# At most three streamed weight loads under way, and one streamed pair moved from the v to the q projection, in a recurrent attention kernel

## The chip, the cores and the metric

The kernel runs on one core of one Trainium2 chip. The metric is the time of one execution on the device in microseconds (us), lower is better. A change counts as faster or slower when it moves the time by more than 2%; verdicts come from several runs with a 95% interval. A ratio below is the mean time of one kernel's fast runs over that of the other's fast runs of the same rounds, so it is not quite the ratio of the medians that are quoted beside it.

Names: PE is the matmul engine, ACT, DVE and POOL are the other compute engines, SP is the engine that issues most of the DMAs here, in program order. The profile prints times in us.

## The reference, cut to what matters

```python
for s in range(n_seg):                         # 64 segments of 32 tokens, one after the other
    xs = x[:, s * 32:(s + 1) * 32, :]
    h = concatenate([mem, xs], axis=1)         # 8 memory rows + 32 rows
    q, k, v = h @ Wq, h @ Wk, h @ Wv           # 1024 -> 32 heads x 128
    p = softmax(where(mask, q k^T * scale, -1e9))
    o = (p v) @ Wo                             # 32 x 128 -> 1024
    mem = o[:, :8, :]                          # the next segment needs this
    outs.append(o[:, 8:, :])
b = gelu(x @ w_gate) * (x @ w_up) @ w_down     # a dense stage, independent of the loop
return g * a + (1 - g) * b                     # a: the concatenated outs; g: a sigmoid gate of x, cut here
```

All in bfloat16. Each segment needs all four weights, 8 MB each, 32 MB in all. That is more than fits on the chip beside the rest. So most of the weights stay resident and a part is streamed from HBM again in every segment.

## The kernel before

The weights are cut into 64 pieces of 512 KB: four matrices, two halves of the heads (r = 0 and 1), eight pieces i. Some pieces share a slot in pairs: piece i of one half and piece i of the other half take turns in one slot. The other pieces stay. There are 12 pairs (k 2, q 2, v 5, o 3), so each segment loads 12 pieces.

```python
PAIRS = {"k": (0, 2), "q": (0, 2), "v": (0, 1, 2, 4, 6), "o": (0, 2, 4)}

def seq(m, r):                       # order of the pieces in one projection half
    p = [i for i in range(8) if i in PAIRS[m]]
    f = sorted(...)                  # the others
    return p + f if r == 0 else f + p
ORDER = (("k", 0), ("q", 0), ("v", 0), ("k", 1), ("q", 1), ("o", 0), ("v", 1), ("o", 1))
walk = [(m, r, i) for m, r in ORDER for i in seq(m, r)]
```

In the first half (r = 0) the paired pieces come first; as soon as PE has used one, SP loads its partner into the slot; the partner is used at the very end of the second half (r = 1). The next segment begins with the half that is then in the slots, so there is one load per pair and segment.

```python
def fetch(n):
    k, t = uses[n][done[n]], slots[n]
    ...
    op("sp", lambda e: e.dma_start(dst(t, k), src(k)), wr=[t.r()], lane=lane)

def spent(k):                        # called after the matmuls that used piece k
    n = home[k]
    done[n] += 1
    if done[n] < len(uses[n]) and uses[n][done[n]] != k:
        fetch(n)
```

`op` works out from the regions read and written (`rd`, `wr`) which semaphores an instruction waits for; `after=` adds such a wait. So a load waits for PE's last use of its slot and for nothing else. One projection piece is 4 matmuls of 512 columns (k, q, v) or 8 of 256 columns (o), on four column groups of the array at once:

```python
for g in range(4):
    ins = e.matmul(PB[bk][32 * g:32 * g + 32, :], lhsT=h[:, i, :], rhs=w[:, g * 512:(g + 1) * 512],
                   start=(p % 8 == 0), stop=(p % 8 == 7))
```

Of the kernel before, what the change touches and what calls it, by code (L numbers as in the profile page):

```python
# [30 lines left out]
class _Prog:  # L31
# [47 lines left out]
    def op(self, eng, fn, rd=(), wr=(), lane=None, after=()):  # L79
        o = _Op(eng, fn)  # L80
        if lane is not None:
            ln = self.lanes.get(lane)
            if ln is None:
                ln = self.lanes[lane] = [self.new_sem(f"{self.name}_{lane}"), 0, None]
            if ln[2] is not None:
                o.deps.append(ln[2])
            ln[1] += 16
            o.sem, o.val, o.inc, o.need = ln[0], ln[1], 16, True
            ln[2] = o
        for r in rd:  # L90
            self._touch(o, r, False, lane is not None)
        for r in wr:
            self._touch(o, r, True, lane is not None)
        o.deps.extend(after)
        if eng == "pool" and lane is None:
            if self.pool is not None:
                o.deps.append(self.pool)
            self.pool = o
        for d in o.deps:
            d.need = True  # L100
        o.idx = len(self.ops)
        self.ops.append(o)
        return o
# [92 lines left out]
def bass_gated_mix__memory_aug_recurrent_mem_tr__geglu_ffn__prompt_kernel(  # L196
# [34 lines left out]
    with ExitStack() as es:  # L231
# [31 lines left out]
        def al(name, shape, dt=BF16, at=None):  # L263
            if at is None:
                cur[0] = (cur[0] + 63) // 64 * 64
                t = _T(nc, name, shape, dt, cur[0])
                cur[0] += t.nb
                return t
            return _T(nc, name, shape, dt, at)
# [12 lines left out]
        kT = al("kT", [128, 4, 4, LQ])  # L282
        qT = al("qT", [128, 4, 4, 32])
# [20 lines left out]
        NSLOT = NLOW + (top - cur[0]) // PIECE  # L304


        PAIRS = {"k": (0, 2), "q": (0, 2), "v": (0, 1, 2, 4, 6), "o": (0, 2, 4)}

        def seq(m, r):
            p = [i for i in range(8) if i in PAIRS[m]]  # L310
            f = sorted((i for i in range(8) if i not in p), key=lambda i: (m == "k" and i % 2, i))
            return p + f if r == 0 else f + p
# [3 lines left out]
        def at_step(p, s):  # L316
            m, r, i = walk[p]
            return (m, r ^ (s % 2), i)

        hosts = []  # L320
        for m in "kqvo":
            for i in range(8):
                if i in PAIRS[m]:
                    hosts.append([(m, 0, i), (m, 1, i)])
# [7 lines left out]
        for s_ in range(NSEG):  # L332
            for p in range(64):
                k = at_step(p, s_)
# [3 lines left out]
        op = P.op  # L338
# [3 lines left out]
        def src(k):  # L342
            m, u, i = k
            if m == "o":
                h0 = 16 * u + 2 * i
                return A_Wo[h0:h0 + 2].rearrange("h p f -> p h f")
            W = {"q": A_Wq, "k": A_Wk, "v": A_Wv}[m]
            return W[i * 128:(i + 1) * 128, 16 * u:16 * u + 16, :].rearrange("d h e -> d (h e)")

        def dst(t, k):  # L350
            return t[:, :].rearrange("p (h f) -> p h f", h=2) if k[0] == "o" else t[:, :]

        nlane = [0]
        done = [0] * len(hosts)

        def fetch(n):
            k, t = uses[n][done[n]], slots[n]
            if paired(k):
                lane = f"sl{n}"
            else:  # L360
                lane = f"res{nlane[0] % 8}"
                nlane[0] += 1
            op("sp", lambda e: e.dma_start(dst(t, k), src(k)), wr=[t.r()], lane=lane)

        def first(k):
            n = home[k]
            if done[n] == 0 and uses[n][0] == k:
                fetch(n)

        def spent(k):  # L370
            n = home[k]
            assert uses[n][done[n]] == k
# [3 lines that stand above are left out]
# [8 lines left out]
        for g in range(4):  # L384
            q = slice(32 * g, 32 * g + 32)
# [68 lines left out]
        def load_qk(s, r):  # L454
            u = r ^ (s % 2)
            op("pool", lambda e: e.dma_start(qkr[:, r, :, :], qk_scr[:, s, 2 * u:2 * u + 2, :]),
               rd=[("D", "qk", s // 4, 2 * u), ("D", "qk", s // 4, 2 * u + 1)], wr=[qkr.r(256 * r, 256 * r + 256)], lane=f"qkr{r}")

        def load_v(s, us=slice(0, 2)):
# [7 lines left out]
           wr=[gwb.r()], lane="gw")  # L467
# [90 lines left out]
        assert NSEG % 2 == 0  # L558
        lost = [("o", 1, i) for i in PAIRS["o"]]
        xo = {k: al(f"xo{k[2]}", [128, 2048], at=tail - (n + 1) * PIECE) for n, k in enumerate(lost)}  # L560
# [17 lines left out]
        def dve_copy(o, i, rd, wr):  # L578
            op("dve", lambda e: e.tensor_copy(o, i), rd=rd, wr=wr)  # L579
# [3 lines left out]
        def evac(bank, t):  # L583
            act_copy(t[:, :], PB[bank][:, :], [BK(bank)], [t.r()])
# [6 lines left out]
        def trans(to):  # L591
            op("pe", trans4, rd=[tok.r(), ident.r()], wr=[BK(TT)])
            i_ap = PBV[TT][:, 0:512].rearrange("p (j g c) -> p (j g) c", g=4, c=32)
            dve_copy(to[:, :, :, 0:32].rearrange("p j g c -> p (j g) c"), i_ap, [BK(TT)], [to.r()])
# [169 lines left out]
        for s in range(NSEG):  # L764
# [12 lines left out]
            def on(m, r, n, *fs):  # L777
                at.setdefault(base_of[m, r] + n, []).extend(fs)
# [27 lines left out]
            on("q", 0, 0, lambda: evac(bank_of["k", 0], tok))  # L806
            on("q", 0, 5, lambda: trans(kT))
            on("v", 0, 0, lambda: evac(bank_of["q", 0], tok))
            on("v", 0, 4, lambda: trans(qT))
            on("k", 1, 0, lambda: evac(bank_of["v", 0], vA))  # L810
            on("k", 1, 0, lambda: scores(0))
            on("k", 1, 3, lambda: rest_k(1))
# [1 line left out]
            if not last:  # L814
                on("q", 1, 0, lambda: load_h(s + 1))
                on("q", 1, 1, lambda: load_qk(s + 1, 0))
                on("v", 1, 2, lambda: load_qk(s + 1, 1))
            on("q", 1, 4, lambda: trans(kT))
            if s % 4 == 0 and Q >= 0:
                on("q", 1, 2, lambda: load_oR(Q, 1))  # L820
            if s % 4 == 1 and Q >= 0:
# [97 lines left out]
        for fb in range(NFB):  # L919
            HB, DN = ((0, 1, 2, 3), (4, 5, 6, 7)) if fb % 2 == 0 else ((4, 5, 6, 7), (0, 1, 2, 3))  # L920
            for j in range(NJ):
# [13 lines left out]
                t = tp[j % 2]  # L935
# [76 lines left out]
```

## Time and profile before

The median was 2304 us. The recurrent stage is some 1520 us of it (62 of the 64 segments, from the first hand-over between segments to the last), the dense stage at the end about 645 us, the start about 140 us. A mean segment, from the trace's records (60 segments; times from the segment's start, in us):

| load | k | k | q | q | v | v | v | v | v | o | o | o | next segment |
|---|---|---|---|---|---|---|---|---|---|---|---|---|---|
| landed | 5.2 | 7.1 | 9.2 | 10.7 | 12.2 | 14.0 | 15.3 | 16.6 | 17.8 | 19.2 | 20.9 | 22.4 | 24.5 |
| first used | 8.1 | 8.4 | 10.4 | 11.0 | 17.8 | 18.0 | 18.3 | 18.5 | 18.9 | 22.6 | 22.9 | 23.3 | |

The stream is almost as long as PE's own work. These lines are from the page of the kernel before; in the rows each digit (or number) is one of 40 equal slices of the span, PE and DMA in tenths of busy time, GB/s as moved:

```profile
span 2304.5 us, 80168 instructions
PE   2588998899999998898998998998879999999998
DMA  9968788788788787787887887887782802606206
GB/s 358 379 213 305 257 304 294 261 289 309 265 303 302 272 316 271 269 322 265 290 323 248 302 302 256 302 303 266 270 330 90 276 34 80 230 1 208 103 1 237
```

Who PE waited for (who <- whom: us in total, times, longest us):

```profile
PE pb L682 <- issue: 46.1, 44, 2.3
...
PE pb L670 <- DMA sl<-in_A_Wq_dram: 18.4, 28, 1.6
...
PE pb L670 <- DMA sl<-in_A_Wv_dram: 7.9, 13, 1.0
...
PE pb L682 <- DMA sl<-in_A_Wo_dram: 7.6, 14, 1.0
```

L670 is a k, q or v projection piece, L682 an o piece. "issue" means that no semaphore explains the wait. The last number of the DMA issue lines is the median time from issue to landing:

```profile
sl<-in_A_Wv_dram SPq DMA_DIRECT2D x331, 512.0 KB, 9.9
sl<-in_A_Wo_dram SPq DMA_DIRECT2D x205, 512.0 KB, 5.9
sl<-in_A_Wk_dram SPq DMA_DIRECT2D x142, 512.0 KB, 5.5
sl<-in_A_Wq_dram SPq DMA_DIRECT2D x142, 512.0 KB, 7.4
```

The v pieces take 9.9 us because up to eight loads wait in line. The last view is the DMA view of one segment, 799.9 to 823.7 us, again in 40 slices (0.6 us each):

```profile
DMA  0037988999999999999999999999999999720120
GB/s 0 0 69 241 220 172 256 407 413 386 379 413 386 399 372 399 379 392 399 386 372 372 386 406 413 427 406 386 358 358 389 392 410 372 282 83 34 34 76 0
```

After a slow start of about 3 us (70 to 256 GB/s) the stream runs at about 390 GB/s until all 12 loads are in.

### The profile page before, as it was taken

To read this page: it belongs to the slowest core of one execution; us is meant where nothing else is said; L and a number is where in the kernel's file an instruction comes from. 1 tells how busy PE (TensorE), PEld (TensorE's weight loads), DVE (VectorE), ACT (ScalarE), POOL (GpSimd) and SP (SyncE) were. 2 spreads that over 40 slices of the span, in tenths; PEclk is the share of its full clock that TensorE was granted. 3 is DMA by queue.
4 is the path that set the end of the run, shared out by engine and by line. 5 is a ranking of instruction groups with operands and counts; after the bars stand their busy time and mean duration, and the time that the engine had idled before them with its cause. 6 is when DMAs were issued, how large, how long until landed. Compare 5 with 4: busy or idle time off the path is not lost.

```text
span 2304.5 us, 80168 instructions
## 1 busy us (share of the span) xinstructions
PE 2060.9 (89%) x36594; PEld 1099.2 (48%) x36614; DVE 901.2 (39%) x2164; ACT 604.1 (26%) x1280; POOL 616.0 (27%) x1107
## 2 busy tenths in 40 slices
PE   2588998899999998898998998998879999999998
PEld 1244555555555555555555455554444444444443
DVE  3134333334334343343343433333335164363452
ACT  1122232222323222232232322222223032131230
POOL 5233333343333433333333333333210000000000
PEclk9999999999999999999999999999999999999999
DMA  9968788788788787787887887887782802606206
GB/s 358 379 213 305 257 304 294 261 289 309 265 303 302 272 316 271 269 322 265 290 323 248 302 302 256 302 303 266 270 330 90 276 34 80 230 1 208 103 1 237
DMA packets 225714, 576.45 MB, mean 250 GB/s; under 512 B 30424, under 2 KB 42584, under 8 KB 225376
## 3 DMA queue, kind: packets, MB, share of 16 engines
q1 hardware_dynamic: 189536, 513.35, 61.7%
q0 software_dynamic: 26624, 44.14, 5.6%
q10 hardware_dynamic: 9216, 13.83, 1.7%
q8 instruction: 287, 4.70, 0.8%
q14 instruction: 51, 0.42, 0.1%
HBM read 539.71 MB, written 31.39 MB: 248 GB/s over the span
## 4 chain that ended last, share of the span: by engine, by line
PE 65%; DMA 24%; issue 5%; DVE 3%; ACT 2%; POOL 1%; SPq 0%; ACTq 0%; POOLq 0%; DVEq 0%
PE pb L670 20%; PE pb L929 14%; DMA sl<-in_A_Wq_dram 11%; PE pb L682 9%; PE pb L697 6%; PE pb L966 6%; DMA sl<-in_A_Wo_dram 5%; PE pb L712 3%; PE pb L588 3%; DMA sl<-in_A_Wv_dram 3%; DMA wd<-in_B_w_down_dram 2%; PE pb L609 1%; DMA xr_scr<-xr 1%; PE pb L641 1%; PE pb L603 1%
## 5 line engine op out<-in xcount | busy, mean ns | idle before, releaser
L670 PE MATMUL pb<-sl,hT 128*32 128x512 bf16 x12288 | 756.8, 383 | 43.2 <-DMA sl<-in_A_Wq_dram 18.4
L670 PEld LDWEIGHTS pb<-sl,hT 128*32 128x32 bf16 x12288 | 331.7, 97 | 327.2 <-DMA sl<-in_A_Wq_dram 38.8
L682 PE MATMUL pb<-sl,oT 128*32 128x256 bf16 x8192 | 281.8, 275 | 56.2 <-issue 46.1
L576 ACT ACTIVATE tok<-pb 128x512 bf16<-128x512 f32 x320 | 191.0, 597 | 458.0 <-PE pb L670 393.0
L682 PEld LDWEIGHTS pb<-sl,oT 128*32 128x32 bf16 x8192 | 213.0, 97 | 98.7 <-issue 54.6
L697 PE MATMUL pb<-sl,hR 128*32 128x512 bf16 x3072 | 215.0, 390 | 19.6 <-DMA sl<-in_A_Wq_dram 7.3
L929 PE MATMUL pb<-xT,wg 128*128 128x512 bf16 x896 | 213.2, 381 | 16.2 <-DVE GT L945 8.4
L655 POOL COPY oRc<-oT 128x128 bf16<-128x128 bf16 x128 | 98.6, 770 | 452.4 <-DVE oT L579 445.4
L929 PE MATMUL pb<-xT,wu 128*128 128x512 bf16 x896 | 211.7, 379 | 0.0
L966 PE MATMUL pb<-wd,GT 128*128 128x512 bf16 x876 | 194.7, 379 | 8.9 <-DMA wd<-in_B_w_down_dram 7.7
L579 DVE CAST oT<-pb 128x160 bf16<-128x160 f32 x256 | 71.2, 320 | 230.4 <-PE pb L646 230.4
L937 ACT ACTIVATE s<-pb 128x512 f32<-128x512 f32 x112 | 66.8, 596 | 326.8 <-PE pb L929 307.3
L929 PEld LDWEIGHTS pb<-xT,wg 128*128 128x128 bf16 x896 | 87.1, 98 | 125.1 <-DVE GT L945 12.8
L576 ACT ACTIVATE vA<-pb 128x512 bf16<-128x512 f32 x128 | 76.4, 597 | 265.9 <-PE pb L670 265.9
L966 PEld LDWEIGHTS pb<-wd,GT 128*128 128x128 bf16 x896 | 86.4, 98 | 117.2 <-DMA wd<-in_B_w_down_dram 15.5
L588 PE MATMUL pb<-ident,tok 128*128 128x128 bf16 x1280 | 128.1, 222 | 13.2 <-ACT tok L576 8.9
L929 PEld LDWEIGHTS pb<-xT,wu 128*128 128x128 bf16 x896 | 87.7, 98 | 105.9 <-issue 0.3
L938 DVE SCALAR_TENSOR_TENSOR tp<-s,pb 128x512 f32<-128x512 f32 x112 | 76.9, 687 | 155.2 <-ACT s L937 155.1
L588 PEld LDWEIGHTS pb<-ident,tok 128*128 128x128 bf16 x1280 | 72.6, 98 | 123.2 <-ACT tok L576 94.3
L579 DVE COPY kT<-pb 128x512 bf16<-128x512 bf16 x128 | 51.9, 405 | 197.9 <-PE pb L588 197.9
L614 DVE TENSOR_REDUCE st<-pb 128x8 f32<-128x320 f32 x128 | 62.9, 492 | 159.6 <-PE pb L609 159.6
L697 PEld LDWEIGHTS pb<-sl,hR 128*32 128x32 bf16 x3072 | 83.3, 98 | 81.5 <-DMA sl<-in_A_Wq_dram 8.4
(76 smaller groups left out, 1929.7 us busy)
## 6 DMA issues: line engine op xcount, KB each, us to landing
sl<-in_A_Wv_dram SPq DMA_DIRECT2D x331, 512.0 KB, 9.9
sl<-in_A_Wo_dram SPq DMA_DIRECT2D x205, 512.0 KB, 5.9
sl<-in_A_Wk_dram SPq DMA_DIRECT2D x142, 512.0 KB, 5.5
sl<-in_A_Wq_dram SPq DMA_DIRECT2D x142, 512.0 KB, 7.4
wd<-in_B_w_down_dram SPq DMA_DIRECT2D x56, 1024.0 KB, 6.4
qk_scr<-stg POOLq DMA_DIRECT2D x64, 128.0 KB, 5.8
qkr<-qk_scr POOLq DMA_DIRECT2D x128, 64.0 KB, 5.4
wg<-in_B_w_gate_dram SPq DMA_DIRECT2D x3, 1792.0 KB, 13.2
```

The source lines that it names most:

```text
L576: op("act", lambda e: e.activation(o, i, ACTF.Copy), rd=rd, wr=wr)
L579: op("dve", lambda e: e.tensor_copy(o, i), rd=rd, wr=wr)
L588: ins = e.transpose(PBV[TT][:, j * 128:(j + 1) * 128], tok[:, j * 128:(j + 1) * 128], ident[:, :])
L655: op("pool", lambda e: e.tensor_copy(oRc[:, u, :, :].rearrange("p c x -> p x c"), oT[:, :, :, 32:40].rearrange("p g j c -> p (g j) c")), r ...
L670: ins = e.matmul(PB[bk][32 * g:32 * g + 32, :], lhsT=h[:, i, :], rhs=w[:, g * 512:(g + 1) * 512], start=(p % 8 == 0), stop=(p % 8 == 7))
L682: ins = e.matmul(PB[XO][32 * g:32 * g + 32, 0:256], lhsT=oT[:, gp_, 2 * jj + hh, 0:32], rhs=w[:, c:c + 256], start=(r == 0 and p % 8 == 0 ...
L697: ins = e.matmul(PB[b][32 * g:32 * g + 32, :], lhsT=h[:, k[2], :], rhs=w[:, g * 512:(g + 1) * 512], start=(n == 0), stop=(n == 7))
L712: ins = e.matmul(PB[b][32 * g:32 * g + 32, 0:256], lhsT=t[:, :, 2 * i + hh], rhs=w[:, c:c + 256], start=(ends[0] and i == 0 and hh == 0), ...
L929: ins = e.matmul(PB[bk][:, 0:FB], lhsT=w[:, kc, cc:cc + 128], rhs=xT[:, :, :, kc, :].rearrange("p t i c -> p (t i) c"), start=(kc == 0), s ...
L937: op("act", lambda e, hg=hg: e.activation(s1[:, :], hg, ACTF.Square, scale=SQ), rd=[BK(bg)], wr=[s1.r()])
L938: op("dve", lambda e, hg=hg, t=t: e.scalar_tensor_tensor(out=t[:, :], in0=s1[:, :], scalar=1.0, in1=hg, op0=ALU.add, op1=ALU.mult), rd=[BK ...
L966: ins = e.matmul(PB[bank[2 * k + hf]][:, :], lhsT=GT[:, j, tb * 128:(tb + 1) * 128], rhs=w[:, jj, hf * 512:(hf + 1) * 512], start=(j == 0) ...
```

## The change

Two intents. First, PE's "issue" waits are late instruction fetches that stand behind weight loads in the DMA engines, so a shorter line of loads should let them through sooner: SP issues a load only when the third last one has landed. Second, one pair moves from v to q (2/3/4/3 in place of 2/2/5/3), with two transposes one piece later.

```diff
--- before.py
+++ after.py
@@ -304,7 +304,7 @@
         NSLOT = NLOW + (top - cur[0]) // PIECE
 
 
-        PAIRS = {"k": (0, 2), "q": (0, 2), "v": (0, 1, 2, 4, 6), "o": (0, 2, 4)}
+        PAIRS = {"k": (0, 2), "q": (0, 2, 4), "v": (0, 2, 4, 6), "o": (0, 2, 4)}
 
         def seq(m, r):
             p = [i for i in range(8) if i in PAIRS[m]]
@@ -352,6 +352,7 @@
 
         nlane = [0]
         done = [0] * len(hosts)
+        flight = []
 
         def fetch(n):
             k, t = uses[n][done[n]], slots[n]
@@ -360,7 +361,8 @@
             else:
                 lane = f"res{nlane[0] % 8}"
                 nlane[0] += 1
-            op("sp", lambda e: e.dma_start(dst(t, k), src(k)), wr=[t.r()], lane=lane)
+            late = done[n] > 0 and len(flight) >= 3
+            flight.append(op("sp", lambda e: e.dma_start(dst(t, k), src(k)), wr=[t.r()], lane=lane, after=[flight[-3]] if late else ()))
 
         def first(k):
             n = home[k]
@@ -806,7 +808,7 @@
             on("q", 0, 0, lambda: evac(bank_of["k", 0], tok))
             on("q", 0, 5, lambda: trans(kT))
             on("v", 0, 0, lambda: evac(bank_of["q", 0], tok))
-            on("v", 0, 4, lambda: trans(qT))
+            on("v", 0, 5, lambda: trans(qT))
             on("k", 1, 0, lambda: evac(bank_of["v", 0], vA))
             on("k", 1, 0, lambda: scores(0))
             on("k", 1, 3, lambda: rest_k(1))
@@ -815,7 +817,7 @@
                 on("q", 1, 0, lambda: load_h(s + 1))
                 on("q", 1, 1, lambda: load_qk(s + 1, 0))
                 on("v", 1, 2, lambda: load_qk(s + 1, 1))
-            on("q", 1, 4, lambda: trans(kT))
+            on("q", 1, 5, lambda: trans(kT))
             if s % 4 == 0 and Q >= 0:
                 on("q", 1, 2, lambda: load_oR(Q, 1))
             if s % 4 == 1 and Q >= 0:
```

## The prediction

> **What bounds it now.** The page gives PE 89% busy and the DMA engines 70 to 80% in slices 4 to 30. These are the 64 recurrent segments, 24.4 us each (spacing of the hand-over transposes, mean of 62). The waits of PE there: "issue" 62 us in 63 waits over 0.3 us (46 us of it before the Wo matmuls), DMA of Wq pieces 18 us, Wv 8, Wo 7, the a_bf copy 13.
>
> The "issue" waits are instruction fetches. Each falls on the same place of a 256-instruction block of the PE stream, 1.3 to 1.5 us after a 16 KB packet of the instruction queue ended. The Trainium skill ("Runtime: NRT & Kernel Launch", Instruction fetch mechanics) says that the sequencer fetches 16 KiB blocks over its own DMA queue while it executes the current one, and calls this mostly hidden; this trace shows it exposed. The packet takes 1.0 us. It starts about 1.0 us after the previous block's boundary with at most one streamed load under way, 2.3 us with three, 2.6 with four, 3.0 with five or more.
>
> Streaming is nearly as tight as PE. In a mean segment the first k load is issued at 0.55 us and the 12 loads land at 5.2, 7.2 (k), 9.2, 10.7 (q), 12.2, 14.0, 15.3, 16.6, 17.8 (v), 19.2, 20.9, 22.4 (o); the next segment begins at 24.4. About half of the segments wait for the second q piece (used at 10.96). The last v piece has a median slack of 1.0 us, the last o piece 0.5. One of the 16 completions of each load comes 0.3 to 1.1 us after the others, so one DMA engine, probably that with the fetches, sets the landings.
>
> **What the change does.** Bytes, loads (12 a segment) and PE work stay.
> - Cap of three. Two loads remain queued when the next is issued, about 2.7 us of work, against 0.9 us from issue to first packet. So the lagging engine should not run dry: landings about as before. The fetch delay falls from 2.6-3.0 to about 2.3 us; 0.4 us off each fetch wait gains about 25 us (estimate).
> - A pair moves from v to q. The fifth load is now the third q piece. It still lands at about 12.1 us, but is used at about 10.9, at the end of the second q projection: each segment waits about 1.2 us more there, 74 us in all (estimate). The Wv and Wo waits (15 us) nearly vanish, because PE comes later and the ninth and twelfth load keep their places.
> - The transposes one piece later: less slack, no cost.
>
> Sum: +74 -15 -25 = +34 us; I lean a little lower, since the fetch gain may be larger.
>
> **Predicted: 2327 us, 8 in 10 between 2270 and 2370.** Faster by over 2%: 0.08; within 2%: 0.67; slower by over 2%: 0.25.
>
> **What would show it.** In the waits of PE: Wq DMA from 18 to about 85 us; Wv and Wo under 5 together; "issue" about 40 us in the stage. SP's wait view: waits for landings of sl loads (23 us now) reach some hundreds. Median time to landing of v falls from 9.9 to about 5 us.
>
> **What would make it wrong.** If the cap makes q land sooner, the q wait is smaller: faster. If fetches start nearly at once behind a short queue, the 62 us vanish: near 2290. If a cap of three lets the lagging engine run dry (landings over 1.6 us apart), o and v waits grow and the loss passes 3%.

## The result, and the profile after

The change took 2502.7 us (median of 4, 2494.7 to 2503.5) against 2303.9 us: ratio 1.0854, 95% interval 1.0822 to 1.0886. It is slower by 8.5%, and outside the predicted range. The page after:

```profile
span 2492.9 us, 80762 instructions
PE   2588888888888888888888888888778999999998
PEclk6699999999999999999999999999999999999999
DMA  9867777878877777877788777777788160613506
GB/s 360 328 211 261 246 260 253 271 245 268 259 249 255 262 253 250 271 261 259 256 266 262 250 259 252 253 249 253 261 261 323 55 234 1 241 46 104 183 1 219
```

The DMA row hardly differs: 7s and 8s, as before. The GB/s row does: about 255 in place of about 290. **The busy share of the DMA engines did not show that they moved less.** PE's waits after (line numbers are two higher):

```profile
PE pb L672 <- DMA sl<-in_A_Wq_dram: 109.1, 93, 3.6
PE pb L684 <- DMA sl<-in_A_Wo_dram: 61.1, 62, 2.4
...
PE pb L684 <- issue: 24.1, 21, 2.6
PE pb L672 <- DMA sl<-in_A_Wv_dram: 18.2, 25, 1.5
```

The "issue" waits fell as hoped, the waits for all three kinds of late pieces rose. DMA issues after, in the same order as before:

```profile
sl<-in_A_Wv_dram SPq DMA_DIRECT2D x268, 512.0 KB, 5.7
...
sl<-in_A_Wo_dram SPq DMA_DIRECT2D x205, 512.0 KB, 5.5
sl<-in_A_Wk_dram SPq DMA_DIRECT2D x142, 512.0 KB, 5.5
```

With three under way a load still takes 5.6 us from issue to landing, whatever it is. Three loads in 5.6 us is one each 1.87 us; the engines had taken one each 1.3 us before. SP's own waits show the cap at work (L143 is the helper's line on which SP now waits for a landing; before, landings of streamed pieces ended 23 us of SP's waits, and none on that line):

```profile
SPq L143 <- DMA sl<-in_A_Wv_dram: 363.4, 246, 8.9
SPq L143 <- DMA sl<-in_A_Wq_dram: 284.0, 192, 3.6
...
SPq L143 <- DMA sl<-in_A_Wk_dram: 238.7, 126, 4.0
```

One segment in the DMA view, 857.5 to 885.7 us, 40 slices of 0.7 us:

```profile
DMA  0048699999998769969997597885679988999102
GB/s 0 0 122 209 186 327 390 384 404 413 352 407 279 227 221 203 198 198 296 325 413 296 192 250 221 261 314 238 110 259 383 305 293 177 299 404 334 67 6 93
```

The slow stretch at the start is the same. But the flat 390 GB/s is gone: the stream falls to 200 GB/s and recovers, again and again. One stretch of these two segments in numbers, from shortly before the v pieces land (the last two numbers are the DMA share and GB/s; a share can pass 1 by a little, as a packet counts where it starts); before:

```profile
806.50:810.00 3.50, 3.50 (x92) 2.01 (x86) 2.51 (x7) 1.37 (x3) 2.15 (x4) 1.00 1.02 387
```

and after:

```profile
866.50:870.00 3.50, 1.80 (x28) 0.59 (x19) 1.86 (x7) 0.29 (x1) 0.00 (x0) 1.00 0.85 208
```

Part of the DMA engines' time is idle after, and the rate fell more than the share. How SP issued in these two segments (start, time from the first to the last issue of the group); before:

```profile
802.11 1.00 SPq L363 DMA_DIRECT2D sl<-in_A_Wq_dram  x2
804.28 2.94 SPq L363 DMA_DIRECT2D sl<-in_A_Wv_dram  x5
```

and after:

```profile
859.76 5.72 SPq L365 DMA_DIRECT2D sl<-in_A_Wq_dram  x3
866.84 6.61 SPq L365 DMA_DIRECT2D sl<-in_A_Wv_dram  x4
```

And what PE saw of it after, at the end of the second q projection (the bracket is idle time and what ended it):

```profile
867.50 0.95 PE L672 MATMUL pb<-sl,hT 128*32 128x512 bf16 x8
872.01 0.40 PE L672 MATMUL pb<-sl,hT 128*32 128x512 bf16 x4 [3.57 <-DMA sl<-in_A_Wq_dram]
```

The third q piece was issued at 865.15 and landed at 871.97; PE stood 3.57 us.

The mean segment after (60 segments): landings at 5.2, 7.1 (k), 9.1, 10.7, 12.7 (q), 14.9, 16.7, 18.5, 20.5 (v), 22.4, 24.3, 26.1 (o), the next segment at 27.4. The first four landings are those of before. From the fifth on each load comes about 1.9 us after the one before, and the last o piece, used the moment it lands, is 3.7 us later than before. 0.9 us of that was slack before, which leaves the 2.9 us by which the segment grew; 62 segments of it are 180 us of the 188 us between the two profiled spans.

### The profile page after: what moved, and what is told of

It is laid out like the page before. It is cut to its first block, busy times and chain, and to the rows that moved or that the text cites. A ratio compares the mean times of both kernels' runs of the same rounds, so it can differ in the third digit from the quotient of the medians.

```text
span 2492.9 us, 80762 instructions
## 1 busy us (share of the span) xinstructions
PE 2125.3 (85%) x36614; PEld 1104.3 (44%) x36614; DVE 901.0 (36%) x2164; ACT 603.6 (24%) x1280; POOL 615.9 (25%) x1107
## 4 chain that ended last, share of the span: by engine, by line
DMA 46%; PE 45%; issue 3%; DVE 3%; ACT 2%; POOL 1%; SPq 0%; ACTq 0%; POOLq 0%
DMA sl<-in_A_Wq_dram 14%; PE pb L931 13%; DMA sl<-in_A_Wo_dram 12%; PE pb L672 11%; DMA sl<-in_A_Wv_dram 9%; DMA sl<-in_A_Wk_dram 8%; PE pb L968 6%; PE pb L684 5%; PE pb L699 3%; PE pb L714 3%; PE pb L590 2%; DMA wd<-in_B_w_down_dram 2%; DMA xr_scr<-xr 1%; POOL gp L443 1%; ACT a_bf L578 1%
## 5 line engine op out<-in xcount | busy, mean ns | idle before, releaser
L672 PE MATMUL pb<-sl,hT 128*32 128x512 bf16 x12288 | 788.3, 390 | 142.9 <-DMA sl<-in_A_Wq_dram 109.1
L672 PEld LDWEIGHTS pb<-sl,hT 128*32 128x32 bf16 x12288 | 340.5, 98 | 453.7 <-DMA sl<-in_A_Wq_dram 143.4
L684 PE MATMUL pb<-sl,oT 128*32 128x256 bf16 x8192 | 290.5, 278 | 87.8 <-DMA sl<-in_A_Wo_dram 61.1
L684 PEld LDWEIGHTS pb<-sl,oT 128*32 128x32 bf16 x8192 | 209.3, 98 | 143.7 <-DMA sl<-in_A_Wo_dram 82.0
L699 PE MATMUL pb<-sl,hR 128*32 128x512 bf16 x3072 | 225.6, 408 | 22.5 <-DMA sl<-in_A_Wq_dram 10.2
```

The costliest lines, as they stand in the source:

```text
L684: ins = e.matmul(PB[XO][32 * g:32 * g + 32, 0:256], lhsT=oT[:, gp_, 2 * jj + hh, 0:32], rhs=w[:, c:c + 256], start=(r == 0 and p % 8 == 0 ...
L699: ins = e.matmul(PB[b][32 * g:32 * g + 32, :], lhsT=h[:, k[2], :], rhs=w[:, g * 512:(g + 1) * 512], start=(n == 0), stop=(n == 7))
```

## The experiments

Theory A: the cap starves the stream; the moved pair is a small extra. Theory B: the moved pair is most of the loss. Within A: what counts is the bytes under way (A1) or the number of DMAs under way (A2), there is a cost per DMA that nothing overlaps (A3), or, for a single load, the engines fall out of step (A4). The text for one load uses A1 for packets that are slow behind a short queue.

### The change without its cap

```diff
-            late = done[n] > 0 and len(flight) >= 3
+            late = False
```

> The change without its cap: pairs 2/3/4/3 and the later transposes, loads issued as soon as their slot is free. Theory A (the cap starves the stream: three loads of 512 KB under way, 5.6 us from issue to landing, give 281 GB/s; the pairs are a small extra): the third q piece lands near 12.1 us after the segment's start, PE waits for it about 1.2 us more in each segment than before, v and o waits vanish: 2350 to 2370 us, landings 1.35 to 1.6 us apart. Theory B (the moved pair is most of the loss, the cap little): 2460 to 2500 us, Wq waits stay near 109 us.

Measured: 2355.7 us, ratio 1.0199 (1.0146 to 1.0251). Third q piece landed at 12.1 and was used at 12.1. PE's waits:

```profile
PE pb L672 <- DMA sl<-in_A_Wq_dram: 79.2, 101, 2.3
PE pb L684 <- issue: 37.8, 36, 2.7
...
PE pb L684 <- DMA sl<-in_A_Wo_dram: 12.7, 16, 2.8
```

So A. The moved pair alone costs 2.0% (verdict unclear, as the interval includes 2%), by the wait for the third q piece (18 to 79 us), as the prediction had costed it. The Wv waits are gone (0.5 us in the stage), the Wo waits are not (7.6 to 12.7 us). Note the "issue" waits: they fall without any cap (46 to 38 us on L684). The likely reason is that PE, held up at q, gives the fetches more time; no run tests this.

### The cap without the moved pair

```diff
-            op("sp", lambda e: e.dma_start(dst(t, k), src(k)), wr=[t.r()], lane=lane)
+            late = done[n] > 0 and len(flight) >= 3
+            flight.append(op("sp", lambda e: e.dma_start(dst(t, k), src(k)), wr=[t.r()], lane=lane,
+                             after=[flight[-3]] if late else ()))
```

> The kernel before with the cap of three alone, pairs 2/2/5/3 and transposes as before. Theory A: the stream of 12 loads is paced at 1.85 to 1.9 us a load whatever the pairs, the last o piece lands near 26 us, segments of 27 us: 2480 to 2510 us, so the pairs add nothing on top of the cap; Wq waits near 20 us, Wv waits 80 us or more. Theory B: 2300 to 2340 us.

Measured: 2485.7 us, ratio 1.0765 (1.0735 to 1.0795), last o piece at 25.9, segments of 27.2 us. PE's waits:

```profile
PE pb L672 <- DMA sl<-in_A_Wv_dram: 133.7, 100, 3.7
PE pb L684 <- DMA sl<-in_A_Wo_dram: 46.4, 54, 2.6
...
PE pb L672 <- DMA sl<-in_A_Wq_dram: 12.0, 26, 1.9
```

So A again. The cap alone costs 7.7% and the moved pair adds only 0.9 points on top of it, not 2.0. The same stream of 12 loads is late either way; the pairs decide only at which piece PE meets the lateness: here at v, in the change at q. SP's own reaction is not what is slow: in the profile after, it issued 0.06 us (median) after the landing that it waited for.

### Four and six under way, with the pairs of the change

```diff
-            late = done[n] > 0 and len(flight) >= 3
+            late = done[n] > 0 and len(flight) >= 4        # or 6
-            ... after=[flight[-3]] if late else ()
+            ... after=[flight[-4]] if late else ()         # or -6
```

> The change with four under way in place of three. Theory A: four loads over some 6 us from issue to landing are about 350 GB/s, nearly what the unlimited stream reaches: landings 1.5 to 1.65 us apart, 2370 to 2410 us. Theory B: as the change, 2480 to 2500 us.

> The change with six under way. Theory A: as without a cap within 1%: 2345 to 2375 us; instruction fetches start as late as before (about 2.6 us after the block's boundary with four or more under way), so their waits are near 60 us again. Theory B: as the change.

Measured: four 2370.6 us, ratio 1.0277 (1.0235 to 1.0320); six 2368.9 us, ratio 1.0257 (1.0191 to 1.0323). Without a cap it was 1.0199. So one more load under way wins back nearly all of the cap's loss, and beyond four there is nothing to gain that these intervals show. The fetch waits were not better than without a cap: all "issue" waits of the stage were 47 us with four, 53 with six, 47 with none.

### Two and one under way

```diff
-            late = done[n] > 0 and len(flight) >= 3
+            late = done[n] > 0 and len(flight) >= 2        # or 1
```

> The change with two under way. If the pace is the time to landing over the number under way, the time to landing falls by less than one load's 1.35 us from 5.6, so 4.3 to 4.8 us over two: 2.15 to 2.4 us a load, last o piece at 29 to 31 us, segments of 30 to 32.5 us, 2660 to 2820 us; instruction fetches start about 1.2 us after the block's boundary and their waits nearly vanish (under 10 us). If three is only slow because of the order of the loads or the moved pair, two should be within 3% of three (2430 to 2580 us).

> The change with one load under way: it measures a load that shares the queue with no other load. Theory A1, slow packets behind a short queue: the time to landing is 4.0 to 4.6 us (with two under way it was 4.7, with three 5.6; the first load of a segment takes 4.6), 4 KB packets take 250 ns or more on average (195 with three, 178 without a cap), segments of 50 to 56 us, 3900 to 4300 us. Theory A4, engines out of step: with one load every engine starts idle, so packets take about 160 to 180 ns and a load lands after 1.0 us to the first packet, 8 packets of 0.16 us and 0.36 us, 2.7 to 3.2 us: segments of 34 to 40 us, 2900 to 3300 us.

Measured in one run each: two 2829.1 us, just above the expected band (last o piece 31.4, segments 32.7); one 3783.6 us, below A1's band and above A4's. The issue lines of the run with two:

```profile
sl<-in_A_Wv_dram SPq DMA_DIRECT2D x268, 512.0 KB, 4.8
```

and of the run with one:

```profile
sl<-in_A_Wv_dram SPq DMA_DIRECT2D x268, 512.0 KB, 3.5
```

**A load that has the queue to itself takes 3.5 us.** In the trace the first packet starts 1.0 us after the issue and the semaphore is complete 0.3 us after the last packet. Between these lie 2.2 us, where eight packets of 160 ns on each of the 16 engines would be 1.3 us: the packets average 201 ns (177 without a cap), and the engines do not start together: the sixteenth packet of a load starts 0.4 us (median) after its first. So the single load lies between the two theories, and both have a part. All runs with the change's pairs side by side; GB/s and busy share are from 200 to 1600 us, "pace" is the spacing of the landings of the v pieces, where the line is longest:

| under way | median us | segment | median issue to landing | landing / number | pace | GB/s | DMA busy |
|---|---|---|---|---|---|---|---|
| no cap | 2355.7 | 25.4 | 7.5 | | 1.27 | 277 | 0.78 |
| 6 | 2368.9 | 25.2 | 7.3 | | 1.30 | 279 | 0.78 |
| 4 | 2370.6 | 25.4 | 6.1 | 1.53 | 1.37 | 276 | 0.79 |
| 3 | 2502.7 | 27.4 | 5.6 | 1.87 | 1.87 | 257 | 0.78 |
| 2 | 2829.1 | 32.7 | 4.8 | 2.40 | 2.57 | 215 | 0.69 |
| 1 | 3783.6 | 47.5 | 3.5 | 3.5 | 3.73 | 148 | 0.46 |

Two of these rows as the profile prints them, window and length, busy time (and count) of PE, PEld (its weight loads), DVE, ACT and POOL, then the granted clock, the DMA share and GB/s. With no cap:

```profile
200.00:1600.00 1400.00, 1259.37 (x29144) 717.40 (x29147) 514.48 (x1474) 393.42 (x895) 496.36 (x919) 0.99 0.78 277
```

and with three:

```profile
200.00:1600.00 1400.00, 1202.69 (x26944) 659.83 (x26940) 475.68 (x1364) 364.68 (x830) 462.57 (x857) 0.97 0.78 257
```

The share is 0.78 in both. Part of the answer is the packets' length: 4 KB packets average 177 ns without a cap and 195 with three under way, so an engine that moves less still counts as busy.

While a cap binds, the pace is about the time to landing over the number of loads under way; that much is arithmetic. What the runs show is that the time to landing grows with the number (3.5, 4.8, 5.6 us), so that three are not enough for the engines' own 1.3 us. Up to three the stream is bound by the time to landing. At four it hardly is: the quotient is still 1.53, but it is a median over all twelve loads, and the pace in the v stretch is 1.37. The fetches did gain: their "issue" waits in the stage were 35 us with three, 3 us with two and 0.2 us with one.

### Halves: the same bytes under way, in smaller steps

```diff
+            for x in range(2 if paired(k) else 1):        # each half has its own semaphore
+                late = done[n] > 0 and len(flight) >= 6   # control: never
+                ...
+                flight.append(op("sp", lambda e, o=o, i=i: e.dma_start(o, i), wr=[wr], lane=ln,
+                                 after=[flight[-6]] if late else ()))
```

> The change with each streamed piece loaded as two halves of 256 KB and six of those under way: the same 1.5 MB under way, but refilled by a sixth and not by a third. Theory A1 (what counts is the bytes under way over the whole time, as the window falls by one whole load between a landing and the next load's first packet, 1.0 us later): pace between those of cap three (1.91 us a piece) and cap four (1.66): 1.70 to 1.85, 2380 to 2460 us. Theory A2 (what counts is the number of DMAs under way): as cap six, 2345 to 2385 us. Theory A3 (a cost for each DMA that is not overlapped): above 2520 us.

> Control: the same halves without a cap, so pairs 2/3/4/3 as in the run without a cap (2356 us). If halving itself costs nothing: 2345 to 2370 us. If twice the DMAs cost by themselves, it is above 2380 and the halves with a cap must be read against this one.

Measured: with the cap 2468.3 us, ratio 1.0692 (1.0662 to 1.0722); without 2455.6 us, ratio 1.0648 (1.0624 to 1.0672). The control failed its expectation: halving costs 4% by itself (2455.6 against 2355.7 us). A half row is 2 KB, so k, q and v need twice the packets, and in the slow start of a segment the third q piece lands at 13.2 us in place of 12.1. The total with the cap is just above A1's range as well, so it decides nothing between A1 and A2. In the v stretch alone, two halves land in 1.58 us with six halves under way and in 1.34 without a cap; whole pieces took 1.87 and 1.27. The finer window holds more of the pace for the same bytes, which fits A1, but with other packets; it stays a hint.

### The two transposes alone

```diff
-            on("v", 0, 4, lambda: trans(qT))
+            on("v", 0, 5, lambda: trans(qT))
-            on("q", 1, 4, lambda: trans(kT))
+            on("q", 1, 5, lambda: trans(kT))
```

> The kernel before with only the two transposes moved one piece later. They keep a slack of one piece (0.21 us) before the scores: 2298 to 2312 us, no wait of the scores matmul for qT over 3 us in all. If they mattered, waits of L603 or L588 grow by 10 us or more.

Measured: 2301.7 us, ratio 1.000 (0.9958 to 1.0042). They cost nothing.

### Two tries at a better kernel

```diff
-        PAIRS = {"k": (0, 2), "q": (0, 2), "v": (0, 1, 2, 4, 6), "o": (0, 2, 4)}
+        PAIRS = {"k": (0, 2), "q": (0,), "v": (0, 1, 2, 3, 4, 6), "o": (0, 2, 4)}
```

> A try at a better kernel: no cap, and the opposite move of the change, one more pair from q to v (2/1/6/3). The fourth load, which half of the segments of the kernel before wait for at the end of the second q projection, becomes a v piece with over 7 us until its use: Wq waits from 18 to under 4 us; the ninth load, last of v, is used up to 0.3 us earlier and its waits grow from 8 to about 15 us: 2285 to 2300 us. If the pairs had no part in the loss: 2300 to 2310 us.

The second try is the run with the cap alone, with 5 in place of 3:

> A try at a better kernel: pairs and transposes as before, five loads under way at most. If the time to landing stays near 5.5 us, five under way would suffice for 1.1 us a load, under the 1.3 us that the engines need, so no landing is later than before; instruction fetches find at most five loads instead of up to eight: their waits fall from 65 to about 55 us: 2290 to 2305 us. If fetch waits and load waits trade against each other, as in the run with pairs 2/1/6/3 (fetch waits up from 65 to 87 us while the Wq waits vanished), the same as before: 2303 to 2315 us.

Measured: pairs 2/1/6/3 2313.8 us, ratio 1.0039 (1.0012 to 1.0067), a miss: the Wq waits vanished in the stage as expected, but its "issue" waits rose from 65 to 87 us. PE came sooner to the o pieces and met there fetches that were no sooner. That the two kinds of wait trade against each other is the reading that fits; this run alone does not prove it. Five under way with the old pairs: 2302.4 us, ratio 0.9976 (0.9941 to 1.0011): the same. Its "issue" waits did not fall as expected (65 us in the stage, as before). No version beat the kernel before.

## Why the prediction was wrong

It said 2327 us, 2270 to 2370; it was 2503.

1. **"Cap of three. Two loads remain queued when the next is issued, about 2.7 us of work, against 0.9 us from issue to first packet. So the lagging engine should not run dry: landings about as before."** This step failed, and with it the total. The cap's term in the sum was -25 us; alone it measured +179 us (2485.7 against 2306.6). From the fifth load on, the landings came 1.9 us apart; in the v stretch without a cap it was 1.3, and the cap alone cost 7.7%. The step took it that two queued loads keep all engines busy until the third one's packets arrive. What the runs show in its place is that a load with three under way takes 5.6 us from issue to landing, which is one load each 1.87 us. One term was mis-sized: the prediction counted 0.9 us, to the first packet, where the run with one load under way gives 3.5 us, of which 1.3 are transfer at full pace, so 2.2 us are not. A hint was at hand: the first k load of a segment was issued at 0.55 and landed at 5.2, 4.6 us with no streamed load ahead of it. The Trainium skill has it too: "DMA: Bandwidth & Descriptors", Anatomy of one DMA, gives about 2.0 us of fixed cost plus bytes over 436 GB/s for loads issued by POOL, an estimate of 3.2 us for 512 KB; SP's loads here took 3.5. But this term alone does not explain the loss. 2.2 us is still less than the 2.7 us of queued work, and 3.5 us over three would be 1.17 us a load, which the engines could not even follow. What the step missed besides is that the time to landing grows from 3.5 to 5.6 us between one load and three, without the engines being busy all the time.
2. The same step looked at the lagging engine only. The 16 completions of one load are spread over 1.8 us (median) with three under way, as they are without a cap, and over 0.6 us with one. When the slowest engine reports, the fastest is 1.8 us into the remaining 2.6 us of work (two loads at 1.3 us, an estimate), the report took 0.3 us more, and the next load's first packet is 1.0 us away. By that estimate the fast engines run dry (3.1 us against 2.6). The traces agree that engines stood idle. Between the first and the last landing of a v piece (62 segments), the kernel before kept the DMA engines busy for 99% of the time and the cap alone for 86%; 4 KB packets averaged 162 and 192 ns, and the landings came 1.41 and 1.96 us apart. So idle engines and longer packets had about equal parts in the slower pace. The longer packets are few: the median is 159 ns in both, but 0.6% of the packets took over 250 ns before and 8% with the cap. In the run with one load the first 16 packets of a v load averaged 244 ns and the last 16 averaged 162. This fits packets that are slow when an idle engine starts again, but it is not shown: the trace does not say which engine took a packet, and no run changes the one without the other.
3. **"each segment waits about 1.2 us more there, 74 us in all"**: right in place and nearly in size. Without the cap the Wq waits rose by 61 us. "The Wv and Wo waits (15 us) nearly vanish" was half right: Wv did, Wo rose by 5 us; in the change, where the cap made every landing late, both rose (18 and 61 us).
4. **"The fetch delay falls from 2.6-3.0 to about 2.3 us; 0.4 us off each fetch wait gains about 25 us"**: right about the delay; that the gain came out near in size is partly luck. With three under way a fetch packet started 2.2 us (median) after the previous block's boundary, with the same count as in the prediction, and the stage's "issue" waits fell from 65 to 35 us. The run without the cap shows that 18 us of these 30 come with the moved pair, so they are not the cap's alone. With the cap alone the waits fell to 26 us. Where PE waits for a load, a late fetch can cost less, and these runs do not separate the two.
5. **"Bytes, loads (12 a segment) and PE work stay."** PE's busy time did not stay: 2060.9 us before, 2125.3 after. The clock records have 4 half-speed stretches in the recurrent stage before and 32 after, each 3.4 to 7 us long. The stage grew by 179 us, of which 120 are PE idle and 58 are PE busy for longer. This is the profile's account, not a cause: in the change each segment ends when the last o piece lands, so most of the slower matmuls ran while PE would have waited anyway.
6. "The transposes one piece later: less slack, no cost": right (ratio 1.000).
7. Under "What would make it wrong" the prediction had "If a cap of three lets the lagging engine run dry (landings over 1.6 us apart), o and v waits grow and the loss passes 3%". The three marks came true: landings 1.9 us apart, longer o and v waits, 8.5%. That it was the lagging engine that ran dry is not shown, and the estimate in point 2 points to the others. The case got little weight (slower by over 2%: 0.25), because the step in point 1 seemed to exclude it.

## What to carry to other kernels

Before you cap the loads under way, divide the measured time from issue to landing at that depth (not the time to the first packet) by the number allowed: if the result is above the spacing at which the engines take loads, the cap is likely to be the new bottleneck, as here at three (5.6/3 = 1.87 us against 1.3). Near the crossing the quotient is too rough to decide: at four it was 1.53, still above 1.3, but the pace was 1.37 and the time (2371 us) near that without a cap (2356 us). So measure there. Read the DMA rate in GB/s and the time between landings rather than the DMA busy share, which was 0.78 with and without the cap. When a stream is the bound, moving a pair from one projection to another only moves the place where PE waits: the two parts cost 7.7% and 2.0% alone and 8.5% together.

## What the Trainium skill lacked or had wrong

- "Runtime: NRT & Kernel Launch", Instruction fetch mechanics, calls the fetch of the next 16 KiB block mostly hidden. Here it was not: 63 waits over 0.3 us, 62 us in all, in the recurrent stage of the kernel before, each 1.3 to 1.5 us after the end of a 16 KB packet that itself takes 1.0 us. No page gives how much later these packets start when weight loads are under way: the median start after the block's boundary was about 1.0 us with no or one load under way and 3.0 us with five (before), and 2.2 us with three (after).
- "DMA: Bandwidth & Descriptors", Latency and other measured facts, gives about 0.6 us to the first byte for DMAs issued by SP. Here the first packet of a segment's first load started 1.0 us after the start of the issuing instruction (median, before and after alike). That instruction takes 0.34 us, so it is 0.66 us after its end, and the figure holds if it counts from there, which the page does not say. A load of 512 KB with no other under way landed after 3.5 us.
- The same page has no rule for how many loads must be under way. Here 512 KB loads needed four for nearly the full rate: landings 1.37 us apart with four, 1.87 with three, 2.57 with two, 3.73 with one, 1.27 without a limit.
- "TensorE: Matmul & The Clock Gate", HAM oscillation, gives the rule that PE should have no idle gap over about 3.4 us. In the profile after, the clock fell to half 32 times in the recurrent stage with single waits of median 1.9 us in or across the 3.4 us before; what these stretches share is that PE was idle for 1.55 us or more of those 3.4 us in sum. In 30 of the 32 no single wait reached 3.4 us, so several shorter waits do it as well (with two under way 100 times, least sum 1.42 us). The sum is no sure sign either: other stretches of 3.4 us with up to 1.9 us idle passed without a fall. No page gives a figure for idle time in sum.
